# A planning edge between GpSimd and VectorE, and redrawn planner constants, in a gated mix of memory attention and a feed-forward block

## The chip, the cores and the metric

The kernel runs on one core of a Trainium2 chip. The metric is the device time of one execution in microseconds (us), as the median of several runs. The core has five engines, each with its own in-order queue: TensorE (PE in the rows; PEld is its weight load), VectorE (DVE), ScalarE (ACT), GpSimd (POOL) and SyncE (SP), which here issues every DMA.

## The reference

```python
def _A_ref(x, wq, wk, wv, wo, beta):          # S 2048, D 448, 16 heads of 28, 4 segments of 512
    q, k, v = heads(x @ wq), heads(x @ wk), heads(x @ wv)
    for s in range(4):
        p = softmax(q[s] @ k[s].T * scale + causal_mask)
        a_dot = p @ v[s]
        a_mem = (phi(q[s]) @ M) / (phi(q[s]) @ z + 1e-6)
        out[s] = gb * a_mem + (1 - gb) * a_dot      # gb = sigmoid(beta), by head
        M, z = M + phi(k[s]).T @ v[s], z + phi(k[s]).sum(rows)
    return concat(out) @ wo
def _B_ref(x, w1, w2):                         # F 1792
    return silu(x @ w1) @ w2
g = sigmoid((x * gate_w).sum(-1, keepdims=True))
return g * _A_ref(...) + (1 - g) * _B_ref(...)
```

## The kernel before

Products of 32-bit operands are made from two halves. ScalarE rounds an operand to its **high half**; the **low half** is the operand minus the high half, and three matmuls (high by high, low by high, high by low) replace one. 448 rows make four chunks c of the contraction, c0 to c3, so one product has 3 + 3 + 3 + 2 = 11 matmuls (`product`, `passes`, L563). The low half of a weight or of x takes two operands from SBUF and is a subtraction on VectorE or GpSimd.

Later stages work in 16 bits and need **scales**. For each of x, wq, wk, wv and so on VectorE first takes the largest magnitudes (`size`, tile `sizes`, L387). Then `scales` works in four steps: VectorE gathers them (`most`, L413), TensorE transposes (L417), VectorE makes a small diagonal (`few`, `diag`, L420 to L424), TensorE spreads it to all partitions (L426), and VectorE writes `up` and `top` (L430, L431). Every 16-bit eviction of a projection (`vt` L903 and L907, `stg` L853 and L855) needs such a scale.

The work has two stages. **Stage one** (`project`, to about 155 us) computes q, k and v by segment from transposed x (`xT`), writes them to DRAM scratch, keeps the memory M, and reads w1 and w2 for their sizes. x of segment 0 comes in four pieces tb of 128 tokens (`xquarter`, L779 high, L783 and L784 low, always on VectorE). `weight` loads wv, wq and wk in four chunks each: ScalarE makes the high half (L819), and the low half (L822) goes to VectorE for wv and to whichever of VectorE and GpSimd the planner chooses for wq and wk. **Stage two** runs the attention of 16 groups of 4 heads (scores L1219 into three PSUM banks `sc`, exp L1224, products with v L1253), the row maxima of a later group (L668, L678), and the feed-forward block in two passes (L563 on `xh`, L1121 on `wb`). For each later segment `x16` loads x again in four transfers through a ring of two buffers `rawf`, and makes 16-bit halves `xh` (high L523 on ScalarE, low L515 or L518). The last pass adds the output projection (`oT`, `wos`), the scaled sum `ya` (L1330) and the result `y` (L1334).

**What sets the order.** The order on each engine is fixed when the program is built, by the list planner `Sched`. Each operation is a `Task` with a planned duration, a list `deps` that it may not be planned ahead of, and a priority; the planner hands out the earliest start, ties by priority. Constants at the head of the file (PRICE, PVP, WOP, WOT, MAXO, HA and so on) are its priorities and hop costs. `self.free` is the planned time from which an engine is free. The program is then written out in that order, engine by engine, and the waits of each instruction are put in by the framework, from the tiles that it reads and writes. In `either` the planner picks the engine:

```python
def either(cols, fn, *deps, **k):
    eng = {"DVE": nc.vector, "POOL": nc.gpsimd}
    return sch.add(("DVE", "POOL"), (0.07 + 0.00104 * cols, 0.1 + 0.00224 * cols), lambda e: fn(eng[e]), deps, port=True, **k)
```

Of the kernel before, what the change touches and what calls it, by code (L numbers as in the profile page):

```python
# [26 lines left out]
TB = L // 128  # L27
# [15 lines left out]
UP = 2.0 ** 14  # L43
DOWN = 2.0 ** -24
TINY = 2.0 ** -40
WOT = 59.67
TUS = 1.6
TLAT = 4.0

HP = 0.18  # L50
HA = 0.2
HD = 0.15
HO = 0.09
HS = 0.14
SLACK = 0.88
LOP = 11.21
LATE = 0.08
FIRST = 120.0
WPRIO = 120.0
MAXO = 66.73  # L60
FULL = 0.111
LOCK = 0.06
RB = "cc"
# [3 lines left out]
VS = 11.08  # L67
NV = 8
XS0 = 1.75
VC = -7.68  # L70
OT1 = 8.22
XS = 6.38
QS = -4.77
KS1 = 0.43
SS = 5.62


# [1 line left out]
    return o + VA + VS * k if o or k > VF else -1.0 + 0.1 * k  # L79


PRICE = 34.19
PVRUNS = [((1, 0), 1)]
PVP = 44.58
FLO = -16.6
FHI = 688.88
WOP = 89.36
SZ = 27.69
SZSTEP = 2.77
XPRIO = 87.67  # L90
# [24 lines left out]
class Sched:  # L115

    HOP = {"PE": 0.2 + HP, "ACT": 0.145 + HA, "DVE": 0.13 + HD, "POOL": 0.1 + HO, "SP": 0.1 + HS}
    SAME = {"PE": 0.0, "ACT": 0.0, "DVE": 0.1, "POOL": 0.1, "SP": 0.0}  # L120

    def __init__(self):
        self.free = {e: 1.0 for e in self.HOP}
        self.cand = {e: [] for e in self.HOP}
        self.count = 0
        self.port = {"DVE": 0.0, "POOL": 0.0}
        self.tail = 1.0
# [116 lines left out]
def infini_mix(ctx: ExitStack, tc: tile.TileContext, x, wq, wk, wv, wo, beta, w1, w2, out):  # L244
    nc = tc.nc
# [54 lines left out]
    def dve(cols, fn, *deps, **k):  # L300
        return sch.add("DVE", 0.07 + 0.00104 * cols, fn, deps, **k)
# [7 lines left out]
# [3 lines that stand above are left out]
# [8 lines left out]
    def start(o, i):  # L320
        return nc.sync.dma_start(o, i)
# [377 lines left out]
    def project():  # L699
# [106 lines left out]
        XC = {}  # L806
        WS = {n: {} for n in "qkv"}

        WLOAD = []

        def weight(name, src, prio, places):
            n = W[name].shape[2]
            for c, (b, first, v) in enumerate(places):
                k = dict(uses=[b], prio=prio + 0.01 * c)

                def v(v=v):
                    return v()[:, :n]
                WLOAD.append(dma(170e3, lambda c=c, v=v: start(v(), src[:, c]), takes=[b] if first else [], **k))
                hi = copy(n, lambda c=c, v=v: nc.scalar.activation(W[name][:, c], v(), AF.Copy), WLOAD[-1], **k)  # L819

                def lo(e, c=c, v=v):
                    e.tensor_sub(W[name][:, 4 + c], v(), raw(W[name][:, c]))  # L822
                if name != "v":
                    j = WQ if name == "q" else WK

                    def w3(v=v):
                        return v().rearrange("p (g e) -> p g e", g=NG)
                    size(j, lambda w3=w3: w3()[:, :, :GW], D, WLOAD[-1], uses=[b], prio=prio + 0.01 * c)
                    size(j + 1, lambda w3=w3: w3()[:, :, GW:], 64, WLOAD[-1], uses=[b], prio=prio + 0.01 * c)
                WS[name][c] = [hi, dve(n, lambda lo=lo: lo(nc.vector), hi, **k) if name == "v" else either(n, lo, hi, **k)]  # L830
                if name == "v":
                    size(WV, v, n, WS[name][c][1], uses=[b], prio=prio + XS0)

# [167 lines left out]
        weight("v", wv, -8.9, places[:4])  # L1001
        for tb in range(TB):
            xquarter(tb, -9 + 0.01 * tb + (0.5 if tb else 0))
        weight("q", wq, -6, places[4:8])
        weight("k", wk, -5, places[8:])
        t_gh = gates()
# [127 lines left out]
    SP, PREV = {}, []  # L1134
# [182 lines left out]
    def last_part(s, tb, ps, lasts, prio):  # L1317
# [8 lines left out]
        PRE.update(o=d1, p=d2)  # L1326
        ft = features(ol, oh, ot, [d1, outer, PRE.get("f")], pr - WOT)
        m = product(lambda: pw.v[:, :D], lambda: passes(wos.v, ot.v, True), D, pr,
# [80 lines left out]
```

## Time and profile before

| what | value |
|---|---|
| median of 3 runs | 558.12 us (557.57 to 558.83) |
| profiled execution, its own time | 557.23 us |
| its span, first to last instruction | 555.5 us |
| TensorE (PE) busy | 541.9 us, 98% |
| VectorE (DVE) busy | 413.6 us, 74% |
| ScalarE (ACT) busy | 399.7 us, 72% |
| GpSimd (POOL) busy | 365.2 us, 66% |
| mean granted TensorE clock | 0.997 |

The profile's page gives busy shares over the whole span; the span here is 1.73 us shorter than the execution's own time, which also holds what lies around it. A wait is read from the time for which an engine was idle before an instruction and from what ended that idle time.

### The profile page before, as it was taken

How to read it: one execution, taken by the hardware profiler on the slowest of the kernel's cores; microseconds unless marked ns; L12 is line 12 of the kernel's file. 1: busy time of each engine (PE TensorE's matmuls, PEld its weight loads, DVE VectorE, ACT ScalarE, POOL GpSimd, SP SyncE). 2: the span in 40 equal slices, each digit the busy share in tenths (PEclk: the TensorE clock that was granted, in tenths of full speed). 3: DMA queues.
4: the chain of work that ended last, by engine and by line, in shares of the span. 5: the costliest groups of instructions: out<-in, count | busy, mean ns of one | idle time of the engine just before them, and what ended most of it. 6: DMA issues, size and time to landing. Idle time of an engine off the chain costs nothing.

```text
span 555.5 us, 11580 instructions
## 1 busy us (share of the span) xinstructions
PE 541.9 (98%) x4007; PEld 340.2 (61%) x4007; DVE 413.6 (74%) x1076; ACT 399.7 (72%) x695; POOL 365.2 (66%) x520
## 2 busy tenths in 40 slices
PE   8799999999999999999999999999999999999997
PEld 5588888888844555555656545565556555555544
DVE  6997998788789966789656888857997228745463
ACT  6467988876656878899778978878998897403140
POOL 5813648637320777999899979998999996212220
PEclk9899999999999999999999999999999999999999
DMA  8479888986775445423344235357302213689972
GB/s 293 153 241 217 229 220 242 224 213 188 216 211 163 130 136 176 122 74 79 108 118 127 68 88 155 108 139 180 90 19 70 69 50 94 226 208 222 251 183 83
DMA packets 91497, 85.87 MB, mean 155 GB/s; under 512 B 55432, under 2 KB 79112, under 8 KB 91440
## 3 DMA queue, kind: packets, MB, share of 16 engines
q1 hardware_dynamic: 91440, 85.15, 55.6%
q8 instruction: 31, 0.51, 0.4%
q14 instruction: 26, 0.21, 0.1%
HBM read 52.60 MB, written 26.09 MB: 142 GB/s over the span
## 4 chain that ended last, share of the span: by engine, by line
PE 84%; POOL 5%; DVE 4%; ACT 3%; DMA 2%; issue 2%; DVEq 0%; POOLq 0%; ACTq 0%
PE mm L563 32%; PE mm L1121 22%; PE sc L563 11%; PE sc L668 5%; PE sc L1219 5%; PE cc L1253 5%; POOL phl L1240 3%; DMA rawf<-in_x_dram 1%; ACT pf L1224 1%; PE cc L973 1%; ACT phl L1236 1%; DVE sizes L387 1%; PE cc L936 1%; DMA xraw<-in_x_dram 1%; PE cc L974 1%
## 5 line engine op out<-in xcount | busy, mean ns | idle before, releaser
L1240 POOL TENSOR_TENSOR phl<-pf,phl 128x384 f16<-128x384 f32 (+1 forms) x192 | 189.2, 1004 | 14.9 <-ACT phl L1236 14.8
L1121 PE MATMUL mm<-wb,ghl 128*128 128x448 f16 (+1 forms) x684 | 148.2, 349 | 0.0
L563 PE MATMUL mm<-xh,wa 128*128 128x512 f16 x572 | 140.3, 379 | 0.0
L1224 ACT ACTIVATE pf<-sc,es 128x512 f32<-128x512 f32 (+1 forms) x192 | 109.6, 620 | 15.7 <-PE sc L1219 12.6
L678 DVE CUSTOM_DVE_ANT_0 sc<-sc,mk 128x384 f32<-128x384 f32 (+1 forms) x192 | 104.6, 572 | 18.0 <-PE sc L668 16.6
L1121 PEld LDWEIGHTS <-ghl 128*128 128x128 f16 x684 | 64.7, 97 | 51.7 <-issue 1.0
L1236 ACT ACTIVATE phl<-pf 128x1280 f16<-128x1280 f32 x64 | 81.4, 1274 | 12.4 <-POOL pf L1230 12.3
L563 PEld LDWEIGHTS <-wa 128*128 128x128 f16 x572 | 53.6, 97 | 53.8 <-issue 0.3
L1219 PE MATMUL sc<-ring 86*128 86x512 f16 (+3 forms) x256 | 58.3, 299 | 2.2 <-ACT pf L1224 1.8
L668 PE MATMUL sc<-ring 84*128 84x128 f16 (+3 forms) x256 | 56.1, 299 | 0.5 <-ACT pf L1224 0.5
L1253 PEld LDWEIGHTS <-phl 128*128 128x128 f16 x1280 | 41.9, 96 | 8.8
L574 POOL TENSOR_TENSOR ol<-ol,ml 128x448 f32<-128x448 f32 x12 | 13.6, 1133 | 51.1 <-DMA ol<-o_scr 42.0
L563 PE MATMUL mm<-xT,wqs 128*128 128x512 f32 x176 | 47.2, 406 | 0.0
L563 PE MATMUL mm<-xT,wks 128*128 128x512 f32 x176 | 45.9, 400 | 0.0
L1098 ACT ACTIVATE th<-mm,ths 128x512 f32<-128x512 f32 x52 | 35.5, 689 | 13.3 <-PE mm L563 13.2
L1253 PE MATMUL cc<-vg,phl 128*128 128x29 f16 (+1 forms) x1280 | 43.6, 182 | 0.0
L1261 DVE TENSOR_REDUCE oraw<-cc 128x116 f32<-128x232 f32 x64 | 25.1, 393 | 23.3 <-PE cc L1253 23.1
L563 PE MATMUL sc<-wvs,xT 128*128 128x450 f32 x176 | 40.4, 373 | 1.0 <-DVE wvs L822 1.0
L1219 PEld LDWEIGHTS <-ring 86*128 86x128 f16 x256 | 24.5, 97 | 26.3 <-issue 3.5
L1227 POOL TENSOR_SCALAR_AFFINE_SELECT pf<-pf 128x128 f32<-128x128 f32 x64 | 20.9, 326 | 27.7 <-ACT pf L1224 25.3
L1104 DVE SCALAR_TENSOR_TENSOR ghl<-mm,ghl 128x512 f16<-128x512 f32 x52 | 35.1, 680 | 5.2 <-ACT ghl L1102 5.1
L1100 DVE SCALAR_TENSOR_TENSOR mm<-th,mm 128x512 f32<-128x512 f32 x52 | 35.4, 691 | 4.1 <-ACT th L1098 4.0
(162 smaller groups left out, 912.1 us busy)
## 6 DMA issues: line engine op xcount, KB each, us to landing
rawf<-in_w_dram SPq DMA_DIRECT2D x26, 256.0 KB
rawf<-in_w_dram SPq DMA_DIRECT2D x28, 224.0 KB
xraw<-in_x_dram SPq DMA_DIRECT2D x16, 256.0 KB
rawf<-in_x_dram SPq DMA_DIRECT2D x16, 256.0 KB
v_scr<-vt SPq DMA_DIRECT2D x16, 232.0 KB
vg<-v_scr SPq DMA_DIRECT2D x16, 232.0 KB
q_scr<-stg SPq DMA_DIRECT2D x16, 224.0 KB
k_scr<-stg SPq DMA_DIRECT2D x16, 224.0 KB
```

Source lines behind the costliest of these rows:

```text
L563: nc.tensor.matmul(ps(), *p[i], start=(i == 0), stop=(i == n - 1))
L668: nc.tensor.matmul(ps.v[:, u:u + n], rg.v[:KS, 0, hh, i * 128:(i + 1) * 128], rg.v[:KS, 1, hh, :n], start=(i > 0), stop=(i > 0 or j == 3), ...
L678: nc.vector.tensor_tensor_reduce(r, r, MK[:, L - n:], 1.0, NEG, OP.add, OP.max, mx.v[:, hh, i:i + 1])
L1098: e1 = sact(L, lambda ps=ps, th=th: nc.scalar.activation(th.v, ps.v, AF.Tanh, scale=ths[:, s:s + 1]), m, takes=[th], uses=[ps], prio=p0)
L1100: e2 = dve(L, lambda ps=ps, th=th: nc.vector.scalar_tensor_tensor(ps.v, th.v, 1.0, ps.v, op0=OP.add, op1=OP.mult), e1, uses=[ps, th], prio=p0)
L1104: e4 = dve(L, lambda ps=ps, g=g: nc.vector.scalar_tensor_tensor(g.v[:, 1], ps.v, DOWN, g.v[:, 0], op0=OP.mult, op1=OP.subtract), e3, uses= ...
L1121: nc.tensor.matmul(ps.v[:, lo:hi], g.v[:, y, sl], w.v[:, z, lo:hi], start=(j == 0 and i == 0), stop=(j == len(fs) - 1 and i == 2))
L1219: nc.tensor.matmul(ps.v[:, e:e + w], rg.v[:KK, 1, hh, j * 128:(j + 1) * 128], rg.v[:KK, 0, hh, j * 128:], start=True, stop=True)
L1224: ex.append(sact(e, lambda b=b, ps=ps, pf=pf, e=e: nc.scalar.activation(pf.v[:, b, :e], ps.v[:, :e], AF.Exp, scale=es[:, s:s + 1]), m, *ex ...
L1236: hi = copy(1280, lambda hl=hl, flat=flat: nc.scalar.activation(hl.v[:, 0], flat(), AF.Copy), *mk, takes=[hl], uses=[pf], prio=p0 + 2)
L1240: low = pool(w - u, lambda hl=hl, flat=flat, u=u, w=w: nc.gpsimd.tensor_sub(hl.v[:, 1, u:w], flat()[:, u:w], hl.v[:, 0, u:w]), low, uses=[ ...
L1253: nc.tensor.matmul(p[:, i, :2 - z], hl.v[:, z, u:u + 128], vg.v[:, j, hh, :2 - z], start=(z == zs[0] and i == 0), stop=(z == zs[-1] and j ...
```

## The change

Three things are edited. `weight` hands the planner four more dependencies for the low halves of wq and wk: the list `XLO`, which is filled with the low halves of x of segment 0 between the calls for wv and wq. The planned time from which SP is free is 2.0 instead of 1.0. Twelve constants are redrawn.

```diff
-WOT = 59.67
+WOT = 69.63
-HA = 0.2
+HA = 0.17
-LOP = 11.21
+LOP = 11.18
-MAXO = 66.73
+MAXO = 68.84
-VC = -7.68
+VC = -7.39
-QS = -4.77
-KS1 = 0.43
+QS = -4.28
+KS1 = -0.23
-PRICE = 34.19
+PRICE = 32.3
-PVP = 44.58
-FLO = -16.6
-FHI = 688.88
-WOP = 89.36
+PVP = 42.88
+FLO = -15.82
+FHI = 689.36
+WOP = 100.18
...
         self.free = {e: 1.0 for e in self.HOP}
+        self.free["SP"] = 2.0
...
+        XLO = []
...
-                WS[name][c] = [hi, dve(n, lambda lo=lo: lo(nc.vector), hi, **k) if name == "v" else either(n, lo, hi, **k)]
+                WS[name][c] = [hi, dve(n, lambda lo=lo: lo(nc.vector), hi, **k) if name == "v" else either(n, lo, hi, *XLO, **k)]
...
             xquarter(tb, -9 + 0.01 * tb + (0.5 if tb else 0))
+        XLO.extend(XC[0, tb][1] for tb in range(TB))
         weight("q", wq, -6, places[4:8])
```

Line numbers of the changed kernel are 1 higher from L124, 3 higher from L811 and 4 higher from L1004 on. The work stays the same; its order changes in thousands of rows, and a few low halves change between VectorE and GpSimd. Three places follow.

GpSimd (POOL), the first low halves of wq and wk with the semaphores that each waits for (DMAHW is a DMA's, Activation is ScalarE's, DVE would be VectorE's). Before:

```order
L755 AFFINE_SELECT maskb<-maskb 128x128 [waits PE_49]
L822 TENSOR_TENSOR wqs<-raw_156,wqs 128x512 [waits DMAHW0_49,Activation_49]
L822 TENSOR_TENSOR wqs<-raw_156,wqs 128x512 [waits DMAHW1_49,Activation_49]
L822 TENSOR_TENSOR wqs<-raw_156,wqs 128x512 [waits DMAHW2_49,Activation_49]
L822 TENSOR_TENSOR wqs<-raw_156,wqs 128x512 [waits DMAHW3_49,Activation_49]
L822 TENSOR_TENSOR wks<-wa,wks 128x512 [waits DMAHW4_49,Activation_49]
```

Now:

```order
L756 AFFINE_SELECT maskb<-maskb 128x128 [waits PE_49]
L825 TENSOR_TENSOR wqs<-raw_178,wqs 128x512 [waits DMAHW0_49,Activation_49]
L825 TENSOR_TENSOR wqs<-raw_178,wqs 128x512 [waits DMAHW1_49,Activation_49]
L825 TENSOR_TENSOR wqs<-raw_178,wqs 128x512 [waits DMAHW2_49,Activation_49]
L825 TENSOR_TENSOR wqs<-raw_178,wqs 128x512 [waits DMAHW3_49,Activation_49]
L825 TENSOR_TENSOR wks<-wa,wks 128x512 [waits DMAHW4_49,Activation_49]
```

Neither the order nor the semaphores moved here.

TensorE (PE), the first products: three v products (x33), q and k of segment 0, and the first scale's transpose (`most`) and spread (`oneb`, `diag`). Before:

```order
L563 MATMUL sc<-wvs,xT_101 128x450 x33
L563 MATMUL mm<-xT_101,wqs 128x512 x6
L417 MATMUL cc<-ident,most 2x128
L563 MATMUL mm<-xT_101,wqs 128x512 x5
L563 MATMUL mm<-xT_101,wks 128x512 x3
L426 LDWEIGHTS oneb
L426 MATMUL cc<-diag_120,oneb 128x2
L563 MATMUL mm<-xT_101,wks 128x512 x3
```

Now:

```order
L564 MATMUL sc<-wvs,xT_101 128x450 x33
L564 MATMUL mm<-xT_101,wqs 128x512 x9
L418 MATMUL cc<-ident,most 2x128
L564 MATMUL mm<-xT_101,wqs 128x512 x5
L564 MATMUL mm<-xT_101,wks 128x512 x3
L427 LDWEIGHTS oneb
L427 MATMUL cc<-diag_120,oneb 128x2
L564 MATMUL mm<-xT_101,wqs 128x512 x3
```

Three matmuls of q (chunk c2) moved ahead of the first transpose.

ScalarE (ACT) in stage two, from the third to the fourth high half of x of segment 1 (`xh`), with exps (`pf`), high halves of the exps (`phl`) and evictions (`pa`) between. Before:

```order
L523 ACTIVATE xh_2146<-rawf,up 128x512
L1224 ACTIVATE pf<-sc_2922,es 128x256
L1160 ACTIVATE pa<-mm_2516,ogs 128x448
L1160 ACTIVATE pa<-mm_2630,ogs 128x448
L1236 ACTIVATE phl<-pf 128x1280
L1224 ACTIVATE pf<-sc_3001,es 128x512
L1224 ACTIVATE pf<-sc_3029,es 128x512
L1160 ACTIVATE pa<-mm_2867,ogs 128x448
L1224 ACTIVATE pf<-sc_3045,es 128x256
L1224 ACTIVATE pf<-sc_3050,es 128x512
L1224 ACTIVATE pf<-sc_3061,es 128x512
L523 ACTIVATE xh_2146<-rawf,up 128x512
```

Now:

```order
L524 ACTIVATE xh_2147<-rawf,up 128x512
L1228 ACTIVATE pf<-sc_2983,es 128x256
L1164 ACTIVATE pa<-mm_2583,ogs 128x448
L1240 ACTIVATE phl<-pf 128x1280
L1228 ACTIVATE pf<-sc_3045,es 128x512
L1228 ACTIVATE pf<-sc_3048,es 128x512
L1228 ACTIVATE pf<-sc_3053,es 128x256
L1164 ACTIVATE pa<-mm_2723,ogs 128x448
L1164 ACTIVATE pa<-mm_2899,ogs 128x448
L524 ACTIVATE xh_2147<-rawf,up 128x512
```

Eight instructions stand between the two high halves now, and ten before: two exps fewer.

## Rows read from the trace of the kernel before

**Rows 1.** Busy time of each engine in two stretches: us, then PE, PEld, DVE, ACT, POOL, PEclk, DMA
```profile
30.00:155.00 125.00, 124.64 (x677) 104.91 (x676) 107.86 (x284) 96.48 (x208) 62.76 (x103) 1.00 0.83 219
155.00:346.00 191.00, 187.34 (x1626) 104.72 (x1625) 149.67 (x418) 157.68 (x252) 150.04 (x205) 1.00 0.44 125
```
**Rows 2.** What TensorE waited for, whole span: us in total, times, longest
```profile
PE sc L1219 <- ACT pf L1224: 1.8, 2, 1.4
...
PE sc L664 <- ACT pf L1224: 0.9, 1, 0.9
PE sc L668 <- ACT pf L1224: 0.5, 1, 0.5
```
**Rows 3.** Timeline of TensorE, the first 36 us: start, length, instruction, [idle before <-releaser]
```profile
14.79 1.53 PE L563 MATMUL mm<-xT,wqs 128*128 128x512 f32 x6
19.98 0.37 PE L417 MATMUL cc<-ident,most 128*2 128x128 f32 x1 [3.65 <-DVE most L413]
...
23.27 0.17 PE L426 MATMUL cc<-diag,oneb 2*128 2x2 bf16 x1
...
27.36 0.27 PE L417 MATMUL cc<-ident,most 128*2 128x128 f32 x1
...
29.48 0.16 PE L426 MATMUL cc<-diag,oneb 2*128 2x2 bf16 x1
...
30.29 0.27 PE L417 MATMUL cc<-ident,most 128*2 128x128 f32 x1
```
**Rows 4.** Window of TensorE after the idle: us, PE busy, granted clock, DMA, GB/s
```profile
20.00:23.00 3.00, 3.00 (x9) 0.55 0.75 170
```
**Rows 5.** Timeline of VectorE, 10 to 33 us
```profile
10.26 0.29 DVE L784 TENSOR_TENSOR xT<-xraw,xT 64x128 fp32r<-64x128 f32 x1
10.58 0.56 DVE L783 TENSOR_TENSOR xT<-xraw,xT 128x384 fp32r<-128x384 f32 x1
...
14.05 1.27 DVE L784 TENSOR_TENSOR xT<-xraw,xT 64x128 fp32r<-64x128 f32 x1
...
19.77 0.15 DVE L413 TENSOR_REDUCE most<-sizes 128x2 f32<-128x8 f32 x1
...
21.80 0.85 DVE L424 TENSOR_SCALAR diag<-identb,few 2x2 bf16<-2x2 bf16 x1
...
26.21 0.14 DVE L413 TENSOR_REDUCE most<-sizes 128x2 f32<-128x8 f32 x1
26.28 1.26 DVE L907 SCALAR_TENSOR_TENSOR vt<-sc,sv,vt 128x448 f16<-128x448 f32 x2
...
28.33 1.10 DVE L424 TENSOR_SCALAR diag<-identb,few 2x2 bf16<-2x2 bf16 x1
...
29.94 0.14 DVE L413 TENSOR_REDUCE most<-sizes 128x2 f32<-128x8 f32 x1
...
32.35 0.22 DVE L424 TENSOR_SCALAR diag<-identb,few 2x2 bf16<-2x2 bf16 x1
```
**Rows 6.** Timeline of GpSimd, 8 to 36 us
```profile
10.91 5.56 POOL L822 TENSOR_TENSOR wqs<-raw,wqs 128x512 fp32r<-128x512 f32 x4 [3.38 <-ACT wqs L819]
...
28.11 1.30 POOL L802 TENSOR_TENSOR xT<-xraw,xT 64x512 fp32r<-64x512 f32 x1 [2.99 <-issue]
```
**Rows 7.** Timeline of ScalarE, the first evictions of v
```profile
24.36 1.69 ACT L903 ACTIVATE vt<-sc,sv 128x448 f16<-128x448 f32 x3 [6.89 <-DVE sv L454]
```
**Rows 8.** Timeline of all engines, the end of the program
```profile
550.97 0.74 PE L1121 MATMUL mm<-wb,ghl 128*128 128x224 f16 x6
551.17 0.68 DVE L1330 SCALAR_TENSOR_TENSOR ya<-sc,gas,pl 128x448 f32<-128x448 f32 x1 [2.91 <-PE sc L563]
551.94 0.81 DVE L1334 SCALAR_TENSOR_TENSOR y<-mm,ogs,ya 128x224 f32<-128x224 f32 x2
```
**Rows 9.** Timeline of all engines, the fourth transfer of x of segment 1
```profile
216.93 0.33 SPq L321 DMA_DIRECT2D rawf<-in_x_dram  x1
...
220.78 0.72 ACT L523 ACTIVATE xh<-rawf,up 128x512 f16<-128x512 f32 x1 [0.84 <-DMA rawf<-in_x_dram]
```

## The prediction

> **What bounds the kernel now.** I read the busy time by stretches first, then what TensorE waited for, then the timelines where it waited. From 30 to 155 us TensorE is busy 124.64 of 125.0 us, and from 155 to 346 us 187.34 of 191.0 [rows 1]; the page gives it 98% of the whole span. So TensorE's own work is the bound, and an order can only win back its idle time, its slow clock, and the head and tail of the program. The idle time lies in three places. The largest wait stands at the start: TensorE stops 3.65 us in front of the first transpose, released by VectorE's `most` [rows 3]. After it the clock is low: from 20 to 23 us the granted clock is 0.55 of full speed, part of the time at 1.2 and part at 2.4 GHz [rows 4], so this window costs another 3.0 x 0.45 = 1.35 us. In stage two TensorE waits for ScalarE's exps, 1.8 + 0.9 + 0.5 = 3.2 us in five waits [rows 2]. And at the end the last `ya` and two halves of `y` follow the last matmul [rows 8].
>
> **The wait that the change names.** GpSimd starts its low halves of wq at 10.91 us [rows 6], while VectorE still has low halves of x to make. A pair of these takes 0.29 and 0.56 us before that; afterwards a 0.29 us one takes 1.27 us [rows 5]. Two pairs from 10.58 us would end at 10.58 + 2 x 0.86 = 12.3 us; they end at 14.05 + 1.27 = 15.32 us, 3.0 us late. The Trainium skill, page "SBUF — State Buffer", section "Who interferes with whom", says that a VectorE instruction with two SBUF inputs and a GpSimd instruction that reads SBUF exclude each other, and that the loser blocks for the whole instruction; by that rule a GpSimd that waited would give the 3.0 us back. But the new dependencies are the planner's alone. They decide where an instruction is put in its queue, and GpSimd's queue is the same row by row, with the same semaphores: a DMA's and ScalarE's, none of VectorE. ScalarE still makes the first high half of wq before the same point of its queue. So GpSimd starts at 10.9 us again, VectorE is held up again, and `most` ends at 19.92 us again [rows 5]. I cost the edge itself at nothing on these two engines. The edit of SP's planned start issues no instruction either; both only move what the planner puts where.
>
> **The start, step by step.** What does move is TensorE's order.
> 1. Nine matmuls of q stand before the first transpose instead of six. A product matmul takes 0.23 us: 17 of them fill 23.44 to 27.36 us [rows 3]. Three run inside the wait, which shrinks to 3.65 - 0.69 = 2.95 us. Their low halves are there: GpSimd's four end at 16.47 us [rows 6], 1.39 us each, so the third at 15.1.
> 2. From the first to the second transpose 24 product matmuls stand now instead of 25. With the same slow clock the second transpose comes at 27.36 - 0.23 = 27.1 us, and no q work is left behind it. VectorE's `most` for it ends at 26.35 us [rows 5], so it is not late. If the clock stays high, since TensorE stood still for less time, up to 1.35 us could be saved here, but VectorE holds the middle: its `diag` ends at 22.65 and `most` at 26.35 us [rows 5], so TensorE would reach the transpose at 26.5, not sooner.
> 3. Then nine matmuls of v, where six were. VectorE's first `vt` low half is ready at about 26.28 + 0.63 = 26.9 us [rows 5], so they run at 27.4 to 29.4 us.
> 4. Meanwhile `diag` took 1.10 us, because GpSimd's last low half of x of segment 1 ran from 28.11 to 29.41 us [rows 5, 6]; without GpSimd beside it `diag` takes 0.22 us [rows 5]. ScalarE now makes the high half for that one right behind its three `vt`, which end at 26.05 us [rows 7], so GpSimd does it at about 26.7 to 28.0 us and is done before `diag` at 28.2. This saves 0.88 us on VectorE, and the third `most` comes at about 29.2 us instead of 30.08 [rows 5].
> 5. TensorE reaches the third transpose at about 29.9 us instead of 30.29 [rows 3] with two more v matmuls behind it: 0.4 + 2 x 0.22 = 0.8 us ahead.
>
> So the start is worth between 0.8 us (clock as before) and 1.2 us (clock high, steps 2 to 5 moved up by 0.4). I take **0.9 us**, VectorE's lead, because VectorE is busy 107.86 of the next 125 us [rows 1] and will not let TensorE run further ahead for long. The lower bound is nothing: if VectorE's backlog is what paces 30 to 60 us, it can swallow it.
>
> **The end.** Before, six matmuls follow the last output projection, so `ya` (551.17, 0.68 us) stands between it and both halves of `y` (551.94, 0.81 us in all) and VectorE ends at 552.75 us, 1.04 us after the last matmul at 551.71 [rows 8]. Now 27 matmuls of the feed-forward block follow the last projection. At 0.12 us for a half-wide one (0.74 us for six [rows 8]) they take over 3 us: `ya` and the first half of `y` are done under them, and only one half (0.41 us) and its hop remain, about 0.5 us. This is worth **0.55 us**. Bounds: nothing, if a transfer for that projection is late, and 0.6.
>
> **The redrawn rest.** The constants reorder stage two nearly everywhere. What a place in it costs hangs on details that the trace of before shows for the old order only. The waits of 3.2 us [rows 2] hang on one pattern: ScalarE takes the fourth high half of x in its queue, waits for the transfer, and the exps behind it come late. The transfer is issued at 216.93 us, when a buffer comes free, and used at 220.78 us, ScalarE idle 0.84 us before it [rows 9]. In segment 1 two exps fewer stand between the third and the fourth high half now, 1.4 us less cover (an exp takes 0.6 to 0.7 us); in segment 3 nine exps stand there instead of six. One place gets worse and one better, so I take **zero** for stage two. The bounds are the nearest rows: below, the second place's waits vanish (0.9 + 0.5 = 1.4 us gained [rows 2]); above, a whole transfer is exposed once, 220.78 - 216.93 = 3.85 us lost [rows 9]. What hides the transfers of stage one and the work of the other engines is TensorE's dense work [rows 1]; I cost their reordering at nothing too, though with 0.36 us of idle time in 125 us a new order can hardly be better there.
>
> **Sum.** 0.9 + 0.55 = 1.45 us off. Against the profiled execution's own time, 557.23 - 1.45 = 555.78 us. The median of the runs is 0.89 us above that execution, so the forecast for the median is **556.7 us**. A measurement of this kernel can tell about 0.2%, or 1.1 us, from no change: faster means under 557.0, slower over 559.2.
>
> **Rivals.**
> - *The edge works as it is told* (GpSimd does wait, through a semaphore that I overlooked). VectorE's low halves end 3.0 us sooner, `most` at 16.9 us, just when the nine q matmuls end; no idle time, no slow clock. VectorE's chain sets the gain: 558.12 - 3.0 - 0.55 = 554.6 us. For it: the length of the wait. Against it: the semaphore lists. Chance 0.06.
> - *The second place's waits vanish too*: 556.7 - 1.4 = 555.3 us. For it: nine exps of cover in segment 3. Chance 0.20.
> - *Only the tail remains*: VectorE's backlog in 30 to 60 us, or a few new waits in stage one, take back the 0.9 us: 558.12 - 0.55 = 557.6 us, no change. For it: VectorE's load [rows 1]. Chance 0.18.
> - *Slower*: ScalarE's queue is held by the fourth transfer of segment 1. With two exps less of cover and a later issue the whole 3.85 us fall on TensorE, which has three banks of scores and no more to work on: 556.7 + 3.85 = 560.5 us. It decides from 2.6 us of extra waiting on. For it: the excerpt of ScalarE's order and the 1.8 us that this place costs already [rows 2]. Against it: feed-forward matmuls can fill in. Chance 0.16.
>
> **How the numbers follow.** The forecast has 0.40, with a range of its own of 555.8 to 557.6 us (the start between 0 and 1.2, stage two within half a microsecond or so); 0.26 of it lies under 557.0 and 0.14 above. Faster: 0.26 + 0.06 + 0.20 = 0.52. Same: 0.14 + 0.18 = 0.32. Slower: 0.16. The range reaches from 554.4, just beyond the first rival, to 559.6, where most of the slower case is left out.
>
> **What would show it.** Right: GpSimd's first low half of wq starts at 10.9 us, the low half of x beside it takes 1.27 us again, the first transpose stands at 20.0 us with about 2.95 us of idle time before it, the third at about 29.9 us; `diag` of the second scale takes 0.2 us; the last matmul is about 0.5 us before VectorE's end. Wrong: GpSimd starts at 12.4 us (the first rival); or TensorE's waits for `pf` in stage two sum to something far from 3.2 us, which would move the result more than the start does.

## The result and the profile after

The changed kernel takes **559.83 us** (median of 14 runs, 558.13 to 561.31), the kernel before 557.36 us beside it (14 runs, 556.80 to 558.83): ratio **1.0036** (1.0024 to 1.0048), slower by 0.36%, a little more than the 0.2% that can be told from no change. The profiled execution took 560.45 us, span 558.7 us, mean granted clock 0.994 (before 0.997). From its page, the first row:

```profile
PE 544.9 (98%) x4007; PEld 340.7 (61%) x4007; DVE 413.4 (74%) x1077; ACT 400.7 (72%) x695; POOL 367.1 (66%) x520
```

TensorE has the same 4007 matmuls and is busy 3.0 us longer than before (541.9). The span grew by 3.2 us (555.5 to 558.7), so nearly all of it is busy time: the same matmuls took longer, and the idle time of the whole span hardly changed (13.6 to 13.8 us).

The start. Timelines of GpSimd, VectorE and TensorE of the changed kernel (start, length, instruction, idle before), against [rows 3, 5, 6]:

```profile
11.09 5.58 POOL L825 TENSOR_TENSOR wqs<-raw,wqs 128x512 fp32r<-128x512 f32 x4 [2.13 <-ACT gate L908]
14.23 1.27 DVE L785 TENSOR_TENSOR xT<-xraw,xT 64x128 fp32r<-64x128 f32 x1
19.95 0.16 DVE L414 TENSOR_REDUCE most<-sizes 128x2 f32<-128x8 f32 x1
28.55 0.22 DVE L425 TENSOR_SCALAR diag<-identb,few 2x2 bf16<-2x2 bf16 x1
14.81 2.21 PE L564 MATMUL mm<-xT,wqs 128*128 128x512 f32 x9
20.16 0.37 PE L418 MATMUL cc<-ident,most 128*2 128x128 f32 x1 [3.13 <-DVE most L414]
...
30.25 0.27 PE L418 MATMUL cc<-ident,most 128*2 128x128 f32 x1
```

GpSimd does not wait for VectorE; the small low half beside it takes 1.27 us again; nine q matmuls run before the first transpose, and the wait there is 3.13 us instead of 3.65. VectorE's first step on x, the rows of GpSimd and VectorE above and the first transpose all come 0.18 us later in this execution than before; the nine q matmuls start where the six did (14.81 against 14.79 us).

The place where segment 1's x is fetched. SP, ScalarE and TensorE of the changed kernel, against [rows 9] and the L1219 wait of [rows 2]:

```profile
210.36 0.83 SPq L322 DMA_DIRECT2D rawf<-in_x_dram  x2
218.97 0.37 SPq L322 DMA_DIRECT2D rawf<-in_x_dram  x1
213.95 0.72 ACT L524 ACTIVATE xh<-rawf,up 128x512 f16<-128x512 f32 x1 [0.23 <-DMA rawf<-in_x_dram]
216.88 0.72 ACT L524 ACTIVATE xh<-rawf,up 128x512 f16<-128x512 f32 x1 [1.64 <-DMA rawf<-in_x_dram]
218.02 0.49 PE L1223 MATMUL sc<-ring 86*128 86x384 f16 x3 [0.20 <-ACT pf L1228]
220.84 0.38 PE L665 MATMUL sc<-maskb,identb 128*128 128x512 bf16 x1 [0.68 <-ACT pf L1228]
223.15 0.38 PE L1223 MATMUL sc<-ring 86*128 86x384 f16 x2 [0.55 <-DVE mx L679]
224.06 0.27 PE L1223 MATMUL sc<-ring 86*128 86x256 f16 x1 [0.53 <-DVE mx L679]
225.38 0.38 PE L687 MATMUL sc<-ident,mx 128*16 128x128 f32 x1 [0.39 <-ACT pf L1228]
```

The same place in the kernel before:

```profile
207.24 0.96 SPq L321 DMA_DIRECT2D rawf<-in_x_dram  x2
211.95 0.72 ACT L523 ACTIVATE xh<-rawf,up 128x512 f16<-128x512 f32 x1
218.85 0.49 PE L1219 MATMUL sc<-ring 86*128 86x384 f16 x3 [0.32 <-ACT pf L1224]
223.08 0.63 PE L1219 MATMUL sc<-ring 86*128 86x384 f16 x3 [1.45 <-ACT pf L1224]
```

In the changed kernel the second and third quarter are issued together at 210.36 us, 3.1 us later than before. ScalarE stands 1.64 us for the third quarter, and five waits of TensorE sum to 2.35 us, where before two waits of 0.32 and 1.45 us stood. Behind them the clock falls. Windows of TensorE, changed kernel (length, then busy time of PE, PEld, DVE, ACT, POOL, granted clock, DMA share, GB/s):

```profile
220.00:225.00 5.00, 3.17 (x17) 1.32 (x15) 3.22 (x10) 4.97 (x9) 4.62 (x7) 0.98 0.81 224
225.00:230.00 5.00, 4.62 (x36) 2.44 (x37) 2.73 (x9) 3.19 (x6) 5.00 (x7) 0.68 0.07 23
```

0.68 over 5 us is some 3.2 us at 1.2 GHz and the rest at 2.4, and costs 5 x 0.32 = 1.6 us, half of what the span grew by. The same window of the kernel before has a clock of 1.00:

```profile
225.00:230.00 5.00, 5.00 (x46) 2.77 (x44) 3.49 (x12) 4.01 (x8) 4.92 (x8) 1.00 0.38 85
```

Later in stage two the L664 and L668 waits of [rows 2] are gone, and two others, of 0.90 and 0.33 us, stand in the changed kernel instead. In segment 3 ScalarE stands 2.61 us for a quarter of x, longer than in segment 1, but TensorE waits only 0.17 us there, and the clock stays at 1.00 from 320 to 330 us. The last two rows are the tail, against [rows 8]:

```profile
323.62 0.72 ACT L524 ACTIVATE xh<-rawf,up 128x512 f16<-128x512 f32 x1 [2.61 <-DMA rawf<-in_x_dram]
324.97 0.38 PE L1223 MATMUL sc<-ring 86*128 86x512 f16 x1 [0.17 <-ACT pf L1228]
349.49 0.27 PE L1223 MATMUL sc<-ring 86*128 86x256 f16 x1 [0.90 <-ACT pf L1228]
420.85 0.38 PE L1223 MATMUL sc<-ring 86*128 86x384 f16 x2 [0.33 <-DVE mx L679]
...
552.09 3.03 PE L1125 MATMUL mm<-wb,ghl 128*128 128x448 f16 x27
555.16 0.81 DVE L1338 SCALAR_TENSOR_TENSOR y<-mm,ogs,ya 128x224 f32<-128x224 f32 x2 [1.59 <-PE mm L1125]
```

27 matmuls do follow the last projection, but both halves of `y` start only behind the last of them, at 555.16 us.

### The profile page after: what moved, and what is told of

Read it like the earlier page. It is cut to its first block, busy times and chain, and to the rows that moved or that the text cites. A ratio compares the mean times of both kernels' runs of the same rounds, so it can differ in the third digit from the quotient of the medians.

```text
span 558.7 us, 11592 instructions
## 1 busy us (share of the span) xinstructions
PE 544.9 (98%) x4007; PEld 340.7 (61%) x4007; DVE 413.4 (74%) x1077; ACT 400.7 (72%) x695; POOL 367.1 (66%) x520
## 4 chain that ended last, share of the span: by engine, by line
PE 72%; DVE 10%; ACT 6%; POOL 5%; DMA 4%; issue 3%; SPq 0%; DVEq 0%; POOLq 0%; ACTq 0%
PE mm L564 26%; PE mm L1125 19%; PE sc L564 10%; PE sc L1223 5%; PE cc L1257 5%; PE sc L669 4%; POOL phl L1244 3%; DMA rawf<-in_w_dram 2%; DVE sc L679 2%; ACT pf L1228 2%; ACT phl L1240 1%; DMA rawf<-in_x_dram 1%; DVE sizes L388 1%; DMA raw<-in_wv_dram 1%; DVE amr L982 1%
## 5 line engine op out<-in xcount | busy, mean ns | idle before, releaser
L564 PE MATMUL mm<-xh,wa 128*128 128x512 f16 x572 | 143.0, 380 | 0.0
L1223 PE MATMUL sc<-ring 86*128 86x512 f16 (+3 forms) x256 | 59.7, 299 | 3.2 <-DVE mx L679 1.4
L669 PE MATMUL sc<-ring 84*128 84x128 f16 (+3 forms) x256 | 57.6, 301 | 0.0
L575 POOL TENSOR_TENSOR ol<-ol,ml 128x448 f32<-128x448 f32 x12 | 13.8, 1149 | 54.1 <-DMA ol<-o_scr 42.7
L564 PE MATMUL mm<-xT,wks 128*128 128x512 f32 x176 | 47.3, 403 | 0.0
L581 ACT ACTIVATE oh<-ol,os 128x448 f16<-128x448 f32 x16 | 10.5, 664 | 37.3 <-POOL ol L575 35.8
```

What stands on the lines that cost most here:

```text
L564: nc.tensor.matmul(ps(), *p[i], start=(i == 0), stop=(i == n - 1))
L669: nc.tensor.matmul(ps.v[:, u:u + n], rg.v[:KS, 0, hh, i * 128:(i + 1) * 128], rg.v[:KS, 1, hh, :n], start=(i > 0), stop=(i > 0 or j == 3), ...
L1223: nc.tensor.matmul(ps.v[:, e:e + w], rg.v[:KK, 1, hh, j * 128:(j + 1) * 128], rg.v[:KK, 0, hh, j * 128:], start=True, stop=True)
```

## Experiments

All of them replay a fixed order from a table of (step, engine) pairs in place of the planner; stage one is its first 1000 steps. So single steps can be moved. Lines in their profiles are some 60 higher. Every ratio is against the kernel before on the same chip in the same session, and the steps moved are given as the rows of an engine's queue.

| run | order, stage one / two | edit | median us | ratio (95%) |
|---|---|---|---|---|
| e1 | after / before | none | 557.18 | 0.9997 (0.9984 to 1.0011) |
| e2 | before / after | none | 562.51 | 1.0074 (1.0057 to 1.0091) |
| e0 | after / after | none | 559.26 | 1.0010 (0.9990 to 1.0029) |
| e13 | after / after | none | 559.24 | 1.0019 (1.0001 to 1.0037) |
| e3 | before / before | real wait | 554.70 | 0.9951 (0.9934 to 0.9968) |
| e4 | after / after | real wait | 556.28 | 0.9979 (0.9965 to 0.9993) |
| e6 | after / after | four steps back | 557.79 | 1.0004 (0.9990 to 1.0018) |
| e14 | after / after | four steps back | 558.79 | 1.0010 (0.9996 to 1.0023) |
| e12 | after / after | two of the four back | 558.56 | 1.0002 (0.9978 to 1.0026) |
| e10 | before / before | one step late | 558.39 | 1.0015 (1.0006 to 1.0024) |
| e15 | after / after | ScalarE's step alone | 557.36 | 0.9987 (0.9975 to 1.0000) |
| e7 | after / after | wait, four steps | 554.43 | 0.9942 (0.9929 to 0.9956) |
| e8 | after / after | e7 and the fourth quarter | 555.62 | 0.9954 (0.9935 to 0.9972) |
| e9 | after / after | two PSUM tiles at the end | 557.56 | one run |
| e11 | after / after | e7, tiles, one exp | 555.03 | 0.9927 (0.9898 to 0.9956) |
| e16 | after / after | wait, ScalarE's step, tiles, one exp | **553.40** | 0.9926 (0.9907 to 0.9945) |
| e17 | after / after | e16 and four steps | 554.57 | 0.9953 (0.9940 to 0.9965) |

### Which stage loses (e1, e2)

```diff
-order = after[:1000] + after[1000:]
+order = after[:1000] + before[1000:]   # e1
+order = before[:1000] + after[1000:]   # e2
```

Expected of e1: 

> The changed kernel's order in stage one, the order of the kernel before in stage two, both replayed from a table. Theory (what the change loses, it loses in stage two, at the place where segment 1's x is fetched, 210 to 228 us): this kernel is at the time of the kernel before, 557.0 to 557.8 us, ratio 0.999 to 1.001. Rival (stage one as it is now, with 0.18 us more before the first projection and 0.30 us more at 154 us, carries the loss on): 558.5 us or more.

Expected of e2: 

> The order of the kernel before in stage one, the changed kernel's order in stage two. Theory (stage two loses): 559.2 to 560.0 us, ratio 1.003 to 1.005, PE's clock falls again between 225 and 230 us. Rival (stage one loses): 557.0 to 557.8 us.

e1 is at the time of the kernel before, e2 slower than the changed kernel itself. So the loss is in stage two's order, and beside stage two's old order stage one's new order is worth nothing that can be measured. The two stages do not simply add, though: beside stage two's new order e2, with the old stage one, stands at 1.0074 (1.0057 to 1.0091), and the changed order with the new one at 1.0010 to 1.0036 in its three measurements. In e2's profile the clock is 0.66 at 225 to 230 us. Why e2 loses more than the changed kernel stays open: its profiled execution took 559.87 us, the least of its six.

### A real wait (e3, e4)

```diff
+    tie = const.tile([128, 1], F32, name="tie")
...
                 def lo(e, c=c, v=v):
+                    if name == "q" and c == 0:
+                        e.tensor_copy(tie[REM:128], raw(XT[0].v[REM:128, NC, L - 1:]))
                     e.tensor_sub(W[name][:, 4 + c], v(), raw(W[name][:, c]))
```

Expected of e3: 

> The order of the kernel before, and one more instruction on GpSimd: a copy of one column that VectorE's last low half of the first x writes, ahead of the first low half of wq, so that GpSimd really waits for VectorE. Theory (the two engines slow each other where VectorE reads two operands): VectorE's eight subtractions of the first x end near 12.5 us in place of 15.3, the sizes are ready near 17 in place of 19.9, the first projection's last matmuls wait for the fourth low half of wq at 18.1 instead, and the time is 554.3 to 555.5 us, ratio 0.994 to 0.997. Rival (GpSimd is then 1.5 us late with the low halves of wq, wk and segment 1's x, and the queue of VectorE is as full as before): 557 us or more.

Expected of e4: 

> The changed kernel's order with the same extra copy on GpSimd, so that GpSimd waits for VectorE's low halves of the first x. Theory (the copy is worth 2.8 us whatever stage two's order is): 556.6 to 557.6 us, ratio 0.998 to 1.000. Rival (stage two's place at 210 to 228 us takes part of it back, because a chain behind a transfer does not shift with PE): 558 us or more.

e3 gains 557.54 - 554.70 = 2.84 us. Timelines of GpSimd, VectorE and TensorE of e3, then its window after the first transpose. The last two rows are one and the same step near the end of stage one, in e3 and in the kernel before:

```profile
12.67 0.19 POOL L885 COPY tie<-xT 64x1 f32<-64x1 f32 x1 [5.01 <-DVE xT L846]
12.94 5.05 POOL L886 TENSOR_TENSOR wqs<-raw,wqs 128x512 fp32r<-128x512 f32 x4
12.21 0.29 DVE L846 TENSOR_TENSOR xT<-xraw,xT 64x128 fp32r<-64x128 f32 x1
16.96 0.15 DVE L475 TENSOR_REDUCE most<-sizes 128x2 f32<-128x8 f32 x1
17.16 0.27 PE L479 MATMUL cc<-ident,most 128*2 128x128 f32 x1 [0.73 <-DVE most L475]
151.10 0.32 PE L1038 MATMUL cc<-mhl,phq 112*128 112x116 f32 x1 [0.33 <-POOL phq L942]
...
154.08 0.32 PE L974 MATMUL cc<-mhl,phq 112*128 112x116 f32 x1 [0.33 <-POOL phq L878]
```

```profile
20.00:23.00 3.00, 2.87 (x12) 1.83 (x11) 3.00 (x14) 1.69 (x3) 3.00 (x4) 1.00 0.68 262
```

VectorE's last small low half takes 0.29 us, `most` stands at 16.96 us in place of 19.77 [rows 5], TensorE waits 0.73 us instead of 3.65 [rows 3], and the row at 151 us is 2.98 us earlier. That the two engines hold each other up here is thereby shown. A rival is the slow clock behind the first transpose (0.55 at 20 to 23 us [rows 4]), which e3 does not have. It is ruled out by e10 below: its stage one is that of the kernel before, its clock is 1.00 there as well, and the same step stands at 153.86 us, 2.76 us behind e3's. The rule of the Trainium skill that the prediction named (page "SBUF — State Buffer", section "Who interferes with whom") agrees with this trace: with GpSimd waiting, VectorE's last low half of x ends at 12.50 us instead of 15.32, 2.82 us sooner, where the prediction had 3.0. The four low halves of wq take 5.05 us here and 5.56 [rows 6] beside VectorE's subtractions, so GpSimd paid too. In e4 the same copy stands on the changed kernel's order: 0.9979, against 1.0010 to 1.0036 for that order without it, a gain of 1.7 to 3.2 us across chips. The rival (558 us or more) is ruled out.

### The four steps of segment 1's x (e6, e14 and the control; e12; e10)

On VectorE's and SP's queues, e6 against the changed kernel (`wb`, `xh`: low halves of the last down weight and of segment 1's first quarter; `rawf<-in_x_dram`: second and third quarter):

```diff
+wb<-rawf,up,wb 128x448
+xh<-rawf,up,xh 128x512
 mhl<-sc,mhl 16x128
 (three reductions, one sum)
-wb<-rawf,up,wb 128x448
-xh<-rawf,up,xh 128x512
...
+DMA rawf<-in_x_dram 128x512 x2
 DMA m_scr<-mhl 16x2x128
 DMA ring<-m_scr 2x2048
 DMA ring<-q_scr 56x2048
-DMA rawf<-in_x_dram 128x512 x2
```

Expected of e6: 

> The changed kernel's order with four steps moved back to where they stood before: VectorE's low half of the last down weight and of the first quarter of segment 1's x ahead of the maxima's low half and the reductions behind it, and the transfers of the second and third quarter ahead of the maxima's stores and loads on SP's queue. Theory (ScalarE's wait of 1.64 us for the third quarter, and the lower clock at 225 to 230 us that follows PE's idle time, come from these steps): the two transfers start near 206 us in place of 210.4, ScalarE's wait for them is gone, the clock at 225 to 230 us is 1.00, and the time is 557.3 to 558.3 us, ratio 1.000 to 1.002. Rival (PE's idle time there has another releaser, the weighted values and maxima in the redrawn order): no change against the changed kernel, 559.3 to 560.3 us.

Against the kernel before in its session, e6 had none of the loss (1.0004). Its transfers start at 204.60 us and ScalarE's wait for them is gone. From the place on, its order is the changed kernel's row for row, so rows can be matched. First two rows of the changed kernel, then the same two of e6, and e6's clock:

```profile
214.27 0.68 PE L1257 MATMUL cc<-vg,phl 128*128 128x29 f16 x20
...
234.63 0.38 PE L665 MATMUL sc<-maskb,identb 128*128 128x512 bf16 x1
```

```profile
213.94 0.68 PE L1318 MATMUL cc<-vg,phl 128*128 128x29 f16 x20
...
223.33 0.27 PE L1284 MATMUL sc<-ring 86*128 86x256 f16 x1 [1.32 <-ACT pf L1289]
...
232.07 0.38 PE L726 MATMUL sc<-maskb,identb 128*128 128x512 bf16 x1
```

```profile
225.00:230.00 5.00, 5.00 (x63) 2.98 (x61) 3.96 (x13) 4.04 (x8) 5.00 (x8) 1.00 0.29 73
```

The two executions are 0.33 us apart at the first row and 2.56 at the last: the place is worth 2.2 us between them. TensorE's idle time hardly differs, 2.21 us in e6 (0.35, 0.54, 1.32) against 2.35; the clock does, 1.00 against 0.68. Between single executions this shows what the fall costs, not what brings it. And the changed kernel's order, replayed on another chip, gave only 1.0010 (e0), so it was run as a control (e13) beside the order of e6 (e14).

Expected of e0: 

> The changed kernel's own order, replayed from the table that the other runs are cut from: a control. If replaying costs nothing: 559.2 to 560.4 us, ratio 1.002 to 1.005. If the replay itself takes or gives time, the runs before this one have to be read against it.

Expected of e13: 

> The changed kernel's own order, replayed, as the control for the two runs beside it. If its loss is in its order: ratio 1.001 to 1.005, and PE's clock falls at 220 to 230 us in the profile.

Expected of e14: 

> The four steps of segment 1's x moved back, beside the control on one chip. Theory (they make the loss): 1.0 to 2.5 us below the control. Rival (the loss is a clock that falls by chance, the same with and without them): within 0.6 us of the control.

e13's profile has the fall, deeper than in the changed kernel's own profile:

```profile
220.00:225.00 5.00, 3.16 (x18) 1.53 (x16) 3.00 (x11) 4.50 (x8) 3.99 (x7) 0.87 0.66 198
225.00:230.00 5.00, 4.91 (x32) 2.09 (x31) 2.31 (x8) 3.78 (x6) 4.94 (x7) 0.50 0.22 70
```

e14's has none, yet its median is only 0.45 us lower, and their intervals overlap. So the four steps are not shown to make the loss; beside the real wait they are worth 1.85 us (e7 against e4, below).

The two VectorE steps alone, with SP as in the changed kernel:

Expected of e12: 

> The changed kernel's order, with the two VectorE steps alone moved back (the low halves of the last down weight and of segment 1's first quarter of x); the two transfers keep their place on SP's queue, behind the stores of the maxima and the first load for the next ones. Theory A (VectorE's order held the transfers): they start near 206 us and the time is that of the run with all four steps, 557.3 to 558.3 us. Theory B (SP's queue holds them as well, behind the maxima's load, which could not start before 209 us): they start at 209 us or later and the time is 558.8 us or more.

SP's queue of e12:

```profile
209.73 0.31 SPq L383 DMA_DIRECT2D ring<-q_scr  x1
210.13 0.83 SPq L383 DMA_DIRECT2D rawf<-in_x_dram  x2
```

The transfers start as late as in the changed kernel although VectorE is done with their buffers 4.7 us sooner (204.67 and 205.99 us against 209.35 and 210.68). SP holds them: the load of q right ahead of them (`ring<-q_scr`) is issued only at 209.73 us. That is theory B, with the load of q behind the maxima's as the one that holds. In time the run is unclear, and it does not tell the theories apart there.

The same first quarter's low half and transfers put late in the order of the kernel before:

```diff
-xh<-rawf,up,xh 128x512
 oraw<-cc 128x116
 mhl<-sc,mhl 16x128
 (three reductions)
+xh<-rawf,up,xh 128x512
...
-DMA rawf<-in_x_dram 128x512 x2
 DMA m_scr<-mhl 16x2x128
+DMA rawf<-in_x_dram 128x512 x2
```

Expected of e10: 

> The order of the kernel before with one step of the change alone: VectorE's low half of the first quarter of segment 1's x behind the maxima's low half and three groups of reductions, and the two transfers that follow it on SP's queue behind the store of the maxima; all else as before. Theory (that step makes the loss): the two transfers start near 209.8 us in place of 207.2, ScalarE waits 2 to 5 us for them, and the time is 558.6 to 560.3 us, ratio 1.002 to 1.005. Rival (the loss comes from other steps of the redrawn order): 557.0 to 557.8 us.

e10 loses 558.39 - 557.69 = 0.7 us, less than the least expected, in a profile without any fall (clock 1.00 throughout, waits of 1.09, 0.59 and 1.10 us at the place). Here late transfers alone cost waits of that size (2.78 us, 1.0 more than the 1.77 of the kernel before). That the rest of the changed kernel's loss needs the fall of the clock is argued from this, not shown.

### ScalarE's step alone (e15)

On ScalarE's queue; VectorE's low half of the same quarter goes behind one more sum and its reciprocal:

```diff
-xh<-rawf,up 128x512
 pf<-sc,es 128x256
 pa<-mm,ogs 128x448
 phl<-pf 128x1280
+xh<-rawf,up 128x512
```

Expected of e15: 

> The changed kernel's order with the transfers as late as they are, and ScalarE's high half of the third quarter of segment 1's x behind four softmax and eviction steps that do not need it (VectorE's low half of it behind two more steps). Theory (the late transfer costs through ScalarE's queue, which stands 1.64 us for it, and PE then waits 0.68 us for a softmax step at 221 us): the 0.68 and 0.20 us go, and the time is 0.8 to 2.0 us below the control. Rival (PE's waits move on to the next step, and the clock falls anyway): within 0.6 us of the control.

e15 is 1.88 us below the control on the same chip (0.9987, to 1.0000, against 1.0019, from 1.0001), and 2.0 us in the means of 12 runs each. Its transfers are as late as ever (210.55 us). Timelines of ScalarE and TensorE and a window of e15:

```profile
218.63 0.71 ACT L585 ACTIVATE xh<-rawf,up 128x512 f16<-128x512 f32 x1
222.27 0.38 PE L1284 MATMUL sc<-ring 86*128 86x384 f16 x2 [0.55 <-DVE mx L740]
223.18 0.27 PE L1284 MATMUL sc<-ring 86*128 86x256 f16 x1 [0.53 <-DVE mx L740]
224.30 0.28 PE L748 MATMUL sc<-ident,mx 128*16 128x128 f32 x1 [0.21 <-ACT pf L1289]
```

```profile
225.00:230.00 5.00, 5.00 (x63) 2.97 (x61) 3.67 (x13) 4.14 (x8) 5.00 (x7) 1.00 0.24 71
```

The third quarter is there when ScalarE comes to it; TensorE's waits of 0.20 and 0.68 us in front are gone, 1.29 us of idle time is left, and the clock stays at 1.00. That the two steps moved here take the loss back is shown by time. That the loss came from ScalarE standing for the late transfer is argued from these rows, and two other runs speak against that as the whole of it. In e14 ScalarE stands for neither the second nor the third quarter, and it is not shown to be faster than the control. In e0's profile, of the control's order, ScalarE waits 0.74 us for the second quarter and not at all for the third, and the clock falls all the same, to 0.50 at 225 to 230 us.

### The fourth quarter, the tail, and the best version (e7, e8, e9, e11, e16, e17)

Expected of e7: 

> The changed kernel's order with the four steps of segment 1's x moved back and the extra copy on GpSimd. Theory (the two causes are apart and add up, 2.0 and 2.8 us off the changed kernel): 554.5 to 555.5 us, ratio 0.994 to 0.997. Rival (PE's lower clock comes back elsewhere, since PE still idles some 2.2 us at 220 to 224 us): 556.5 us or more.

Expected of e8: 

> As the run with the four steps moved back and the copy, and also the fourth quarter of segment 1's x: VectorE's low half of the second quarter goes ahead of two weighted-value sums, the fourth transfer right behind it, and ScalarE's high half of it ahead of two evictions. Theory (ScalarE's softmax steps that PE waits 1.32 us for at 223 us stand behind the fourth quarter): 0.4 to 1.0 us below the run without it, 553.7 to 554.8 us. Rival (PE then waits for the reductions and softmax in place of it, as long): no difference, 554.5 to 555.5 us.

e7 adds the two gains as expected, though its profiled execution (555.70 us, its slowest) has a clock of 0.67 at 220 to 225 us. e8 moves three more steps:

```diff
+xh<-rawf,up,xh 128x512          # VectorE, second quarter, low half
 oraw<-cc 128x116
 (two reductions)
-xh<-rawf,up,xh 128x512
...
+DMA rawf<-in_x_dram 128x512     # SP, fourth quarter
 DMA ring<-k_scr 28x2048
 DMA p_scr<-pa 128x448
-DMA rawf<-in_x_dram 128x512
...
+xh<-rawf,up 128x512             # ScalarE, fourth quarter, high half
 pa<-mm,ogs 128x448 x2
-xh<-rawf,up 128x512
```

It gains nothing, and TensorE still waits 1.29 us at that row: the theory is ruled out.

e9 gives the second half of the last output rows a PSUM tile of its own:

```diff
             for lo, hi in halves:
+                if lo:
+                    ps = Buf(BK["mm"])
```

Expected of e9: 

> The changed kernel's planner and order (replayed), with a PSUM tile of its own for the second half of the last output rows. Theory (both halves of y waited for the last matmul because they read one tile): the first half's y starts 1.0 to 1.3 us before the last matmul ends, and VectorE's end stands 0.40 to 0.50 us behind the last matmul's end in place of 0.85. Rival (the first half waits for something else, the sums of the attention part): 0.85 us as before.

The tail of e9:

```profile
549.68 3.03 PE L1188 MATMUL mm<-wb,ghl 128*128 128x448 f16 x27
551.60 0.45 DVE L1401 SCALAR_TENSOR_TENSOR y<-mm,ogs,ya 128x224 f32<-128x224 f32 x1 [0.44 <-PE mm L1188]
552.75 0.45 DVE L1401 SCALAR_TENSOR_TENSOR y<-mm,ogs,ya 128x224 f32<-128x224 f32 x1 [0.70 <-PE mm L1188]
```

With a tile of its own the first half starts 1.11 us before the last matmul ends (552.71), and VectorE ends at 553.20, 0.49 us behind it. So both halves had waited because they read one tile.

For e11 one exp of ScalarE (`pf`) is also put ahead of the packing (`phl`) behind which it stood when TensorE waited 0.90 us at 349 us. e16 and e17 take the parts that gained:

```diff
-phl<-pf 128x1280
 pf<-sc,es 128x512
+phl<-pf 128x1280
```

Expected of e11: 

> The parts that gained, together: the changed kernel's order with the four steps of segment 1's x moved back, the extra copy on GpSimd, a PSUM tile of its own for the last half, and one softmax step of ScalarE moved ahead of the packing of the weights, where PE waited 0.90 us at 349 us. Theory (they add up): 553.0 to 554.2 us, ratio 0.991 to 0.995, and the wait of 0.9 us is under 0.3. Rival (the wait moves on to the packed weights, which come 0.6 us later): 554.0 to 555.0 us.

Expected of e16: 

> What gained, together, with ScalarE's step in place of the four: the changed kernel's order with the high half of segment 1's third quarter behind the steps that do not need it, the extra copy on GpSimd, a PSUM tile of its own for the last half, and the softmax step at 349 us moved ahead of the packing. Theory (the clock falls at segment 1's x because ScalarE's queue stands for the late quarter): no fall at 217 to 228 us, and 552.8 to 553.8 us, ratio 0.990 to 0.993. Rival (with the start 3 us earlier the clock falls there as in the runs that have the copy and the four steps): 554.3 us or more.

Expected of e17: 

> As the run beside it, and the four steps of segment 1's x moved back as well. Theory (ScalarE's step does the work, the four add nothing): within 0.6 us of the run beside it. Rival (both help): 0.6 us or more below it.

The wait of 0.90 us is gone in all three, with two of 0.16 to 0.27 us at 370 us in its place. **e16 has the lowest median, 553.40 us, 0.74% below the kernel before**; by ratio e11, on a slower chip, cannot be told from it (0.9926 and 0.9927). The four steps beside it do not help (e17, 554.57). e16's theory on the clock is ruled out: its profiled execution, its slowest at 555.83 us, has the fall with only 0.54 + 0.53 + 0.17 us of idle time:

```profile
220.00:225.00 5.00, 4.30 (x33) 2.10 (x33) 3.56 (x10) 4.21 (x7) 5.00 (x7) 0.66 0.41 135
```

## Why the prediction was wrong, step by step

- **The edge is the planner's alone: right.** GpSimd started at 11.09 us, VectorE's small low half took 1.27 us, `most` stood at 19.95 us. The price that the rival gave to a real wait, 3.0 us, is close to what e3 measured, 2.84.
- **The start, steps 1 to 5: right in place, wrong in worth.** The first wait is 3.13 us (2.95 told), `diag` 0.22 us (0.2), the third transpose at 30.25 us (29.9, and 0.18 of the difference is the later x) with two more v matmuls behind it. The step that failed is "I take 0.9 us, VectorE's lead". At the row of 154 us (L974 before, 154.08 us) the changed kernel stands at 154.38, e1 at 153.93. TensorE comes to the row in front of it 0.26 us earlier than before (153.22 against 153.48 us), and there it waits 0.88 us for GpSimd's `phq` where it waited 0.33: the lead is swallowed. The stated lower bound, nothing, was the answer, and e1's 0.9997 agrees.
- **The 1.35 us of slow clock at the start: mostly not on the path.** With one and the same stage one, the row of 154 us stands at 153.86 us in e10 (clock 1.00 at 20 to 23 us), at 154.08 in the kernel before (0.55 [rows 4]) and at 154.28 in e2 (0.54): 0.2 to 0.4 us of the 1.35. What moved that row by 3 us was VectorE (e3).
- **The end: mis-sized.** 0.55 us told; VectorE ends 0.85 us behind the last matmul (555.97 against 555.12) instead of 1.04, so 0.19 us. The step "the first half of `y` is done under them" failed, and e9 shows why.
- **"I take zero for stage two": this is the step that made the forecast wrong.** "One place gets worse and one better" was right in kind. The better place lost its 0.9 and 0.5 us, but 0.90 and 0.33 us came up elsewhere. The waits for `pf`, which the prediction named as its sign, sum to 2.34 us instead of 3.2 (four waits before, where the prediction counts five, and the one of 0.32 us, at 218.85, comes ahead of the fourth high half and so is not of its pattern). Those for VectorE's `mx` sum to 1.41 instead of 0.27. So as waits alone stage two grew by only some 0.3 us in the profile. The step failed because it priced stage two by its waits and gave TensorE's clock there no term; in the profile a fall of 1.6 us came with the worse place, and e15, which moves ScalarE's step there, is 1.88 us below its control. The worse place was the one that the slower rival named, ScalarE's queue held by a transfer of segment 1's x; but it was the third quarter and not the fourth, which waits for nothing (222.87 us), and 1.64 us of waiting and not 3.85. That this rival's 560.5 us lies near 559.83 is luck. The prediction counted exps between the third and fourth high half and did not look at the two low halves on VectorE and the loads on SP's queue that put the transfers 3 us later.
- **What no step had: the clock in stage two.** Over the three sets of the changed kernel's order (the first measurement, e0, e13) 25 of 38 runs have a mean granted clock under 0.995. Of the 48 runs of e6, e12, e14 and e15, which only move steps at segment 1's x, 16 do, and of the 109 runs of the kernel before beside the experiments 32. On the chips of e0 and e13 the changed kernel's order is not slower than the kernel before in runs at 0.995 or more (means 558.04 us of 5 runs against 558.40 of 11, and 557.86 of 4 against 557.90 of 21). In the others it is: 560.41 against 559.62, and 560.26 against 558.98. So on these two chips the loss stands in the runs in which the clock fell more. In the first measurement, where the clocks of the kernel before are not known, the four runs of the changed kernel at 0.997 still take 558.86 us against 557.56 in the mean of all 14 before, so a share of the waits stays possible. Where the clock fell in runs without a profile cannot be seen; in the profiled ones it fell at the start or at segment 1's x, and nowhere else before the last microseconds.

What stays open: what decides whether the clock falls at segment 1's x. It fell in the profiled executions of the changed kernel, e0, e2, e4, e7, e8, e9, e11, e13 and e16, not in e6, e12, e14, e15 and e17, and in none of the four with stage two's order of before (the kernel itself, e1, e3, e10). Without the real wait there is a pattern in these single executions: all five with stage two's new order untouched have the fall (the changed kernel, e0, e2, e9, e13), and none of the four with steps moved at segment 1's x (e6, e12, e14, e15). With the real wait, some 3 us earlier, five of the six with stage two's new order have it, moved steps or not (e17 has none). The idle time does not decide: 2.78 us without a fall (e10), 1.24 with one (e16). e6 and e14, one order, lie 1.0 us apart in median on two chips.

## What to carry to other kernels

A dependency told to a planner is no wait on the chip: read the semaphores before you price it, and if the wait is worth having, make the engine read something that the other one writes last. When an order is redrawn, follow each transfer back to the step that frees its buffer and to what stands ahead of it in the issuing queue, and look at who stands behind the instruction that first waits for it: an in-order engine that waits for data not yet needed holds up work that is. What that costs hangs on the place: 2.61 us of it in segment 3 cost TensorE a wait of 0.17 us. And give halves that are to be read apart tiles of their own.

## What the hardware showed that was not expected

- A fall of TensorE's clock costs by where it comes. At 20 to 23 us (0.54 and 0.55 against 1.00) the 1.35 us left 0.2 to 0.4 at 154 us. At segment 1's x it costs more: e7's two executions with a mean clock of 1.000 took 553.51 and 553.63 us, its profiled one, with a fall there, 555.70.
- One order on one chip gives both: of e13's 12 runs four lie at 0.997 (557.16 to 558.22 us), the others at 0.987 to 0.994 (559.02 to 562.27 us). A 0.2% verdict on such a kernel is also a count of falls.
- VectorE's reductions are not held up by GpSimd: in the kernel before a 128x512 one takes 0.68 us beside GpSimd's low halves of wk (at 18.65 us) and 0.66 with GpSimd idle (at 30.74 us). A 2x2 `diag` beside GpSimd's low halves of x took 1.04 us in e3 and 0.22 without them; it ended at 26.75 us, and the last of those low halves at 26.73.
